# A fused top-k attention and SwiGLU kernel: the softmax weights from Exp of the bare scores, and one VectorE operation that compares, multiplies and sums

## The chip, the cores and the metric

The kernel runs on one core of a Trainium2 chip. The metric is the time of one launch on the device in microseconds (us), lower is better. The core has a TensorE for matrix products (PE in the profile, with its weight loads as PEld), a VectorE (DVE), a ScalarE (ACT), a GpSimd (POOL) and a SyncE (SP) that issues most transfers. Each engine works through its own list of instructions in order; they wait for each other by semaphores.

## The reference

There are 8 batches of 8 heads, 576 queries and keys, and a head dimension of 64. Each query keeps the scores that reach its 32nd largest; their softmax weighs the values. The 4608 x 512 result goes through a SwiGLU block with a hidden size of 1536.

```python
scores = scale * np.matmul(q, k.transpose(0, 1, 3, 2))
kth = np.partition(scores, -top_k, axis=-1)[..., -top_k:-top_k + 1]      # top_k = 32
scores = np.where(scores >= kth, scores, -1000000000.0)
attn = np.exp(scores - np.max(scores, axis=-1, keepdims=True))
attn = attn / (np.sum(attn, axis=-1, keepdims=True) + 1e-09)
x = np.matmul(attn, v)              # then (B, H, S, D) -> (B*S, H*D)
g = x @ w_gate
out = (g * (1.0 / (1.0 + np.exp(-g))) * (x @ w_val)) @ w_out
```

## The kernel before

**Units and turns.** The attention is cut into 160 units: a batch, one of five query tiles, and a pair of heads. Four of the five tiles have 128 queries and give "full" units with two heads of 128 x 576 scores each. The fifth has 64 queries, and packs both heads into one 128 x 576 tile (a "one-head" unit for VectorE). So there are 128 full and 32 one-head units, 288 tiles of 128 x 576 in all. The main loop (`for n in range(NU + 3)`, L747) makes one turn per unit, and each turn writes instructions for several units at different stages.

**The stages of a unit.** `scores` multiplies q by k into PSUM and ScalarE copies the result to the tile `sc` (L308, L313). `select` (L316) finds the 32nd largest score of each row on VectorE: four rounds of MAX8 (L328) with three MATCH_REPLACE8 (L332) between them, in which the eight values found are overwritten by a very low number. A MATCH_REPLACE8 is preceded in the profile by a small MATCH_VALUE_LOAD. The last operation of `select` is the TENSOR_SCALAR of L338: it compares the scores with the 32nd and gives 0 or a penalty. `penalize` (L342) adds the penalty to the scores on GpSimd (L350) and makes the bias of the exponential there (L348). `weigh` (L353) takes the Exp on ScalarE, which also sums it (L359), and adds the 1e-9 (L364). `normalize` (L367) takes the reciprocal on VectorE (L371) and scales the weights on ScalarE (L374). `turn` transposes them on TensorE (L386) and ScalarE copies them out (L387). `values` multiplies by v (L420), and ScalarE copies to `xT` (L436), the input of the SwiGLU block.

**Where the stages stand.** In turn n VectorE does the top-k of unit n. The penalty and Exp of unit n-1 stand at the beginning of turn n, its reciprocal at the end of turn n, its scaling at the start of turn n+1 and its transposes in turn n+1 (`TURN = 2`). The products with v come for two units at a time, for n-4 and n-3 in every even turn n.

**The SwiGLU block** (`feed`) works on 18 blocks of 256 tokens. It is cut into pieces, each a few matmuls, and `pieces(k)` writes up to k pieces into a turn as long as a credit lasts. `share(n)` (L694) sets the credit of a turn, from a fixed budget (7.0, later 6.4) less the cost of the other TensorE work of that turn. ScalarE takes the results out of PSUM and GpSimd multiplies them (L504, L509); these steps wait in the lists `on_act` and `on_pool` until a `flush` writes them. The program order is therefore fixed by hand, and at the end of the kernel every engine is tied to this order. The w matrices are rounded during the first turns by ScalarE, VectorE (L121) and GpSimd (L122, L123).

Of the kernel before, what the change touches and what calls it, by code (L numbers as in the profile page):

```python
# [8 lines left out]
AF = mybir.ActivationFunctionType  # L9
ALU = mybir.AluOpType  # L10
FP32 = mybir.dt.float32
# [4 lines left out]
P = 128  # L16
TOP_K = 32
LOWEST = -3.4028234663852886e38
FAR = -3.0e38
EPS = 1.0e-9  # L20
# [5 lines left out]
def kernel(  # L26
# [37 lines left out]
    nc = tc.nc  # L64
    B, H, S, D = q.shape
# [10 lines left out]
    scale = 1.0 / float(D) ** 0.5  # L76
    assert D == 64 and R == 64 and H * D == DM and DM == 512 and B * S % BLK == 0

    consts = ctx.enter_context(tc.tile_pool(name="consts", bufs=1))
    ld = ctx.enter_context(tc.tile_pool(name="ld", bufs=2))  # L80
    slabs = ctx.enter_context(tc.tile_pool(name="slabs", bufs=4))
    work = ctx.enter_context(tc.tile_pool(name="work", bufs=2))
    small = ctx.enter_context(tc.tile_pool(name="small", bufs=3))
# [9 lines left out]
    for i in range(NV):  # L93
        vt = consts.tile([P, P], FP32, name=f"vlast{i}")
        nc.vector.memset(vt[:], 0.0)
        vlast.append(vt)
    eps = consts.tile([P, 1], FP32, name="eps")
    nc.vector.memset(eps[:], EPS)
    wg = consts.tile([P, KC, DFF], FP32, name="wg")
    wv = consts.tile([P, KC, DFF], FP32, name="wv")  # L100
    wo = consts.tile([P, MC, DM], FP32, name="wo")
# [94 lines left out]
    early = [lambda: None]  # L196
# [4 lines left out]
    def rounding(n):  # L201
        for _ in range(n):
            next(weight, None)
# [68 lines left out]
    state = {}  # L272

    def n_heads(qt):

        return 1 if qt == J else 2
# [39 lines left out]
    def select(n):  # L316

        nh = n_heads(units[n][1])
        sc = state[n]["sc"]
        m = small.tile([P, 2, TOP_K], FP32, tag="m", name="m", bufs=2)  # L320
        heads = [slice(t * S, (t + 1) * S) for t in range(nh)]
        e = work.tile([P, 2 * S], FP32, tag="e", name="e", bufs=3)
        state[n] |= dict(m=m, e=e, heads=heads)
        cur = sc
        rounds = TOP_K // 8
        for r in range(rounds):
            for t, hs in enumerate(heads):
                nc.vector.max(m[:, t, 8 * r : 8 * r + 8], cur[:, hs])  # L328
                yield
            if r < rounds - 1:  # L330
                for t, hs in enumerate(heads):
                    nc.vector.match_replace(  # L332
                        e[:, hs], m[:, t, 8 * r : 8 * r + 8], cur[:, hs], LOWEST
                    )
                    yield
                cur = e
        for t, hs in enumerate(heads):
            nc.vector.tensor_scalar(  # L338
                e[:, hs], sc[:, hs], m[:, t, TOP_K - 1 : TOP_K], FAR, ALU.is_lt, ALU.mult
            )  # L340

    def penalize(n):  # L342

        st = state[n]
        sc, m, e, heads = st.pop("sc"), st.pop("m"), st["e"], st["heads"]
        nh = len(heads)
        bias = small.tile([P, 2], FP32, tag="bias", name="bias")
        nc.gpsimd.tensor_scalar_mul(bias[:, 0:nh], m[:, 0:nh, 0], -scale)  # L348
        every = slice(0, nh * S)
        nc.gpsimd.tensor_tensor(e[:, every], e[:, every], sc[:, every], ALU.add)  # L350
        st["bias"] = bias

    def weigh(n):  # L353

        st = state[n]
        e, heads, bias = st["e"], st["heads"], st.pop("bias")
        tot = small.tile([P, 2], FP32, tag="tot", name="tot")
        for t, hs in enumerate(heads):
            nc.scalar.activation(  # L359
                e[:, hs], e[:, hs], AF.Exp, bias=bias[:, t : t + 1], scale=scale,  # L360
                accum_out=tot[:, t : t + 1],
            )
        nh = len(heads)
        nc.scalar.activation(tot[:, 0:nh], tot[:, 0:nh], AF.Identity, bias=eps[:])  # L364
        st["tot"] = tot

    def normalize(n):  # L367
        st = state[n]
        tot, e, heads = st.pop("tot"), st["e"], st.pop("heads")
        nh = len(heads)  # L370
        nc.vector.reciprocal(tot[:, 0:nh], tot[:, 0:nh])  # L371
        yield
        for t, hs in enumerate(heads):
            nc.scalar.mul(e[:, hs], e[:, hs], tot[:, t : t + 1])  # L374

# [82 lines left out]
    def flush(queue):  # L458
        while queue:
            queue.pop(0)()  # L460
# [201 lines left out]
    NU = len(units)  # L662
# [3 lines left out]
    def piece():  # L666

        if len(on_act) > 1:
            flush(on_act)
        if len(on_pool) > 1:  # L670
            flush(on_pool)
        while True:
            if not current:
                if not todo or done.get(todo[0], 0) < NHP * BLK:
                    return 0
                flush(on_act)
                flush(on_pool)
                current.append(feed(todo.pop(0)))
            cost = next(current[0], 0)
            if cost == 0:  # L680
                current.pop()
                continue
            return cost

    def fetch(n):

        b, qt, hp = units[n]
        i = b * NHP + hp
        if qt == 0:
            yield from prep(i)  # L690
        if qt == J and i + NHP < len(pairs):
            load(i + NHP)

    def share(n):  # L694


        others = 0.0
        costs = [(m, 0.7) for m in scored(n) + valued(n)] + [(n - TURN, 0.6)]
        for m, cost in costs:
            if m >= 0:  # L700
                others += cost * (0.5 if units[m][1] == J else 1)
        if units[n + 3][1] == 0:
            others += 0.6

        beside = 6.4 if T[1] else 7.0
        return beside * n_heads(units[n][1]) / 2 - others

    def scored(n):

        ahead = [n + 1] if n < 2 else [] if n % 2 else [n + 1, n + 2]  # L710
        return [m for m in ahead if m < NU]

    def valued(n):

        behind = [] if n % 2 else [n - 4, n - 3]
        return [m for m in behind if 0 <= m < NU]

    def pieces(n):
        for _ in range(n):
            if credit[0] >= 1:  # L720
                credit[0] -= piece()

    def run(steps):
        for _ in steps:
            pass

    def finish_units(ns):
        values(ns)
        for n in ns:
            b, qt, hp = units[n]  # L730
            if qt == J and b + 1 < B:
                load_v((b + 1) * NHP + hp)
# [8 lines left out]
    load(2)  # L741
    credit = [0.0]
    no = iter(())
    scaled = no
    TURN = 2
    due = [2.0]
    for n in range(NU + 3):  # L747
        nh = n_heads(units[n][1]) if n < NU else 1
        topk = select(n) if n < NU else no
        norm = normalize(n - 1) if 0 <= n - 1 < NU else no  # L750
        nxt = [scores(m) for m in scored(n)]
        ahead = fetch(n + 3 if n else 2) if n + 3 < NU else no

        def dve(k, beside=True):

            for _ in range(k * nh):
                next(topk, None)
                due[0] += 5 / 6 if beside else 0
                if due[0] >= 1:
                    due[0] -= 1  # L760
                    rounding(1)

        if n >= NU - NHP:
            credit[0] = 8.0
        else:
            credit[0] = min(credit[0] + share(n), share(n) + 1)
        flush(on_act)
        if 0 <= n - 1 < NU:
            penalize(n - 1)
        flush(on_pool)  # L770
        run(scaled)
        if nxt:
            run(nxt.pop(0))
        if valued(n):
            finish_units(valued(n))
        if nxt:
            next(nxt[0])
        early[0]()
        if 0 <= n - 1 < NU:
            weigh(n - 1)  # L780
        if nxt:
            run(nxt.pop())


        dve(2, beside=False)
        if n == 0:
            run(ahead)
            load(3)
            ahead = fetch(3)
        if n < NHP:  # L790
            load_v(n)
        pieces(2)
        flush(on_act)
        dve(1)
        dve(1)
        if 0 <= n - TURN < NU:
            run(turn(n - TURN))

        flush(on_pool)
        next(ahead, None)  # L800
        pieces(1)
        next(ahead, None)
        dve(1)
        pieces(1)
        dve(2, beside=False)
        run(topk)
        next(norm, None)
        scaled = norm
        pieces(6)
    while piece():  # L810
        pass
# [48 lines left out]
```

## Time and profile before

| what | us |
|---|---|
| time, median of 3 runs | 1794.11 (1790.79 to 1795.02) |
| profiled execution, its own time | 1794.33 |
| its span, first to last instruction | 1792.1 |
| TensorE busy | 1691.1 (94%) |
| VectorE busy | 1619.1 (90%) |
| ScalarE busy | 1204.8 (67%) |
| GpSimd busy | 1043.2 (58%) |

The span is the profiled execution's first to last instruction; the 2.2 us between it and the execution's own time lie around it. A group line names the line of the code, the engine, the operation, the output tile and its inputs, how often it ran, the busy time and the mean duration of one in ns, and the engine's idle time before it with what ended it. A timeline line has its start and length in us, then the same names; several neighbours of a kind are merged, with their number behind the x.

### The profile page before, as it was taken

To read this page: it belongs to the slowest core of one execution; us is meant where nothing else is said; L and a number is where in the kernel's file an instruction comes from. 1 tells how busy PE (TensorE), PEld (TensorE's weight loads), DVE (VectorE), ACT (ScalarE), POOL (GpSimd) and SP (SyncE) were. 2 spreads that over 40 slices of the span, in tenths; PEclk is the share of its full clock that TensorE was granted. 3 is DMA by queue.
4 is the path that set the end of the run, shared out by engine and by line. 5 is a ranking of instruction groups with operands and counts; after the bars stand their busy time and mean duration, and the time that the engine had idled before them with its cause. 6 is when DMAs were issued, how large, how long until landed. Compare 5 with 4: busy or idle time off the path is not lost.

```text
span 1792.1 us, 30800 instructions
## 1 busy us (share of the span) xinstructions
PE 1691.1 (94%) x11012; PEld 1398.6 (78%) x11012; DVE 1619.1 (90%) x3372; ACT 1204.8 (67%) x2881; POOL 1043.2 (58%) x930
## 2 busy tenths in 40 slices
PE   4558999799999999999999999999999999999999
PEld 3337678688888888888888878888887878888877
DVE  7999999999999999998999999998999989999400
ACT  6778676667667676667666675767676676676431
POOL 4878756455565646565556546555556555656434
PEclk7569999899999999999999999999999999999989
DMA  7433130001200030001200020000300020000000
GB/s 193 128 94 94 32 75 14 13 1 36 60 1 13 2 81 14 13 1 32 64 13 1 13 70 26 1 13 4 92 1 13 1 49 21 13 1 13 1 12 12
DMA packets 109305, 59.66 MB, mean 33 GB/s; under 512 B 88544, under 2 KB 96992, under 8 KB 109152
## 3 DMA queue, kind: packets, MB, share of 16 engines
q1 hardware_dynamic: 108016, 57.37, 12.3%
q8 instruction: 87, 1.43, 0.3%
q14 instruction: 66, 0.54, 0.1%
q10 hardware_dynamic: 1136, 0.33, 0.1%
HBM read 48.23 MB, written 9.44 MB: 32 GB/s over the span
## 4 chain that ended last, share of the span: by engine, by line
PE 79%; DVE 12%; ACT 4%; POOL 3%; issue 1%; DMA 1%; SPq 0%; ACTq 0%; POOLq 0%; DVEq 0%
PE f L476 40%; PE x_ps L562 8%; PE av L420 8%; PE s L308 7%; PE etps L386 6%; PE y_ps L562 5%; DVE m L328 5%; DVE e L332 5%; PE s L294 2%; DVE e L338 1%; PE kqps L263 1%; PE o_ps L522 1%; ACT e L359 1%; POOL e L350 1%; DVE size L121 1%
## 5 line engine op out<-in xcount | busy, mean ns | idle before, releaser
L328 DVE MAX8 m<-e 128x8 f32<-128x576 f32 x864 | 614.9, 747 | 3.3
L350 POOL TENSOR_TENSOR e<-e,sc 128x1152 f32<-128x1152 f32 (+1 forms) x160 | 382.9, 2393 | 131.6 <-DVE tot L371 110.0
L332 DVE MATCH_REPLACE8 e<-m,e 128x576 f32<-128x576 f32 x576 | 423.5, 741 | 0.0
L476 PE MATMUL f<-xT,wg 128*128 128x256 f32 x1728 | 403.9, 383 | 0.0
L476 PE MATMUL f<-xT,wv 128*128 128x256 f32 x1728 | 399.6, 380 | 0.0
L476 PEld LDWEIGHTS f<-xT,wg 128*128 128x128 f32 x1728 | 325.2, 192 | 52.0 <-issue 9.2
L476 PEld LDWEIGHTS f<-xT,wv 128*128 128x128 f32 x1728 | 323.0, 190 | 49.1 <-issue 7.9
L504 POOL TENSOR_TENSOR h<-h,half_g 128x512 f32<-128x512 f32 x108 | 139.7, 1293 | 284.8 <-ACT h L503 283.0
L359 ACT ACTIVATE e<-e,bias 128x576 f32<-128x576 f32 x288 | 221.9, 775 | 113.4 <-POOL e L350 113.3
L386 PE MATMUL etps<-ident,e 128*128 128x128 f32 (+1 forms) x1312 | 185.1, 284 | 48.1 <-ACT e L374 33.5
L374 ACT ACTIVATE e<-e,tot 128x576 f32<-128x576 f32 x288 | 210.7, 780 | 22.1 <-DVE tot L371 21.8
L509 POOL TENSOR_TENSOR h<-h,val 128x512 f32<-128x512 f32 x108 | 139.2, 1289 | 148.0 <-ACT val L508 146.9
L386 PEld LDWEIGHTS etps<-ident,e 128*128 128x128 f32 (+1 forms) x1312 | 157.2, 145 | 80.3 <-POOL e L350 30.1
L308 PE MATMUL s<-kqT 64*128 64x288 f32 x1024 | 181.2, 461 | 37.3 <-ACT sc L313 22.0
L332 DVE MATCH_REPLACE8 e<-m,sc 128x576 f32<-128x576 f32 x288 | 211.6, 741 | 0.0
L328 DVE MAX8 m<-sc 128x8 f32<-128x576 f32 x288 | 202.6, 739 | 9.2 <-ACT sc L313 9.2
L387 ACT COPY et<-etps 128x512 f32<-128x512 f32 (+1 forms) x448 | 182.5, 483 | 36.3 <-PE etps L386 36.2
L338 DVE TENSOR_SCALAR e<-sc,m 128x576 f32<-128x576 f32 x288 | 182.8, 671 | 1.2
L313 ACT COPY sc<-s 128x288 f32<-128x288 f32 x512 | 164.8, 407 | 19.0 <-PE s L308 18.7
L308 PEld LDWEIGHTS s<-kqT 64*128 64x128 f32 x1024 | 102.0, 198 | 85.2 <-ACT sc L313 27.3
L420 PE MATMUL av<-et,v 128*64 128x128 f32 (+1 forms) x2560 | 162.6, 271 | 0.0
L420 PEld LDWEIGHTS av<-et,v 128*64 128x64 f32 x2560 | 140.8, 143 | 7.2 <-issue 3.4
(73 smaller groups left out, 1979.3 us busy)
## 6 DMA issues: line engine op xcount, KB each, us to landing
v<-in_v_dram SPq DMA_DIRECT2D x32, 256.0 KB, 3.2
kq_in<-in_k_dram SPq DMA_DIRECT2D x63, 128.0 KB, 3.0
kq_in<-in_q_dram SPq DMA_DIRECT2D x63, 128.0 KB, 3.2
w<-in_moe_w_gate_dram SPq DMA_DIRECT2D x12, 512.0 KB, 3.8
w<-in_moe_w_val_dram SPq DMA_DIRECT2D x12, 512.0 KB, 3.7
w<-in_moe_w_out_dram SPq DMA_DIRECT2D x12, 512.0 KB, 3.6
out_dram<-o SPq DMA_DIRECT2D x38, 128.0 KB, 2.4
out_dram<-o SPq DMA_DIRECT2D x16, 256.0 KB, 2.4
```

The source lines that it names most:

```text
L308: nc.tensor.matmul(ps[:, 0:half], slab[d, q0 : q0 + P], slab[d, k0 : k0 + half])
L328: nc.vector.max(m[:, t, 8 * r : 8 * r + 8], cur[:, hs])
L332: nc.vector.match_replace(e[:, hs], m[:, t, 8 * r : 8 * r + 8], cur[:, hs], LOWEST)
L338: nc.vector.tensor_scalar(e[:, hs], sc[:, hs], m[:, t, TOP_K - 1 : TOP_K], FAR, ALU.is_lt, ALU.mult)
L350: nc.gpsimd.tensor_tensor(e[:, every], e[:, every], sc[:, every], ALU.add)
L359: nc.scalar.activation(e[:, hs], e[:, hs], AF.Exp, bias=bias[:, t : t + 1], scale=scale, accum_out=tot[:, t : t + 1],)
L374: nc.scalar.mul(e[:, hs], e[:, hs], tot[:, t : t + 1])
L386: nc.tensor.transpose(ps[0:kl, c * P : (c + 1) * P], e[:, k0 : k0 + kl], ident[:])
L387: nc.scalar.copy(et[0:kl, c0 : c0 + cn, :], ps[0:kl, 0 : cn * P].rearrange("p (c j) -> p c j", c=cn),)
L420: nc.tensor.matmul(av[d, i, 0:ql], weights_, moving, start=c == (0 if last else J), stop=c == (J if last else J - 1),)
L476: nc.tensor.matmul(ps[:, i, :], w[:, kc, m * P : (m + 1) * P], x[:, kc, :], start=(kc == 0), stop=(kc == KC - 1),)
L562: nc.tensor.matmul(ps, lhsT, T[i][m], start=m == 0, stop=m == MQ - 1)
```

## The change

The scores are exponentiated without the penalty, for all 576 keys, on ScalarE while VectorE is still looking for the 32nd largest: `weigh(n)` moves into turn n, behind the first round of MAX8, which gives the largest score for the bias. The top-k rounds get a tile of their own, `rest`, since `e` now holds the exponentials. The last operation of `select` becomes a `scalar_tensor_tensor` with two tensor inputs: it compares the scores with the 32nd, multiplies the 0 or 1 by the exponential and writes the row's sum to `tot`. The penalty's addition on GpSimd is gone, and so are the sum and the addition of 1e-9 on ScalarE; the latter becomes a small GpSimd operation. The reciprocal and the scaling of unit n-1 move to turn n, behind two VectorE operations per head, and its transposes to turn n (`TURN = 1`). The products with v are for n-3 and n-2, in odd turns, and the scores for two units are also made in odd turns. In even turns three pieces of the SwiGLU block stand ahead of the transposes in place of two.

```diff
-    eps = consts.tile([P, 1], FP32, name="eps")
-    nc.vector.memset(eps[:], EPS)
...
+        rest = work.tile([P, 2 * S], FP32, tag="rest", name="rest", bufs=1)
         e = work.tile([P, 2 * S], FP32, tag="e", name="e", bufs=3)
+        tot = small.tile([P, 2], FP32, tag="tot", name="tot")
...
                     nc.vector.match_replace(
-                        e[:, hs], m[:, t, 8 * r : 8 * r + 8], cur[:, hs], LOWEST
+                        rest[:, hs], m[:, t, 8 * r : 8 * r + 8], cur[:, hs], LOWEST
                     )
...
-            nc.vector.tensor_scalar(
-                e[:, hs], sc[:, hs], m[:, t, TOP_K - 1 : TOP_K], FAR, ALU.is_lt, ALU.mult
+            nc.vector.scalar_tensor_tensor(
+                e[:, hs], sc[:, hs], m[:, t, TOP_K - 1 : TOP_K], e[:, hs],
+                ALU.is_ge, ALU.mult, accum_out=tot[:, t : t + 1],
             )
...
-    def penalize(n):
+    def weigh(n):
...
         nc.gpsimd.tensor_scalar_mul(bias[:, 0:nh], m[:, 0:nh, 0], -scale)
-        every = slice(0, nh * S)
-        nc.gpsimd.tensor_tensor(e[:, every], e[:, every], sc[:, every], ALU.add)
...
             nc.scalar.activation(
-                e[:, hs], e[:, hs], AF.Exp, bias=bias[:, t : t + 1], scale=scale,
-                accum_out=tot[:, t : t + 1],
+                e[:, hs], sc[:, hs], AF.Exp, bias=bias[:, t : t + 1], scale=scale
             )
-        nh = len(heads)
-        nc.scalar.activation(tot[:, 0:nh], tot[:, 0:nh], AF.Identity, bias=eps[:])
...
     def normalize(n):
...
+        nc.gpsimd.tensor_scalar_add(tot[:, 0:nh], tot[:, 0:nh], EPS)
+        yield
         nc.vector.reciprocal(tot[:, 0:nh], tot[:, 0:nh])
-        yield
         for t, hs in enumerate(heads):
             nc.scalar.mul(e[:, hs], e[:, hs], tot[:, t : t + 1])
...
-        ahead = [n + 1] if n < 2 else [] if n % 2 else [n + 1, n + 2]
+        ahead = [n + 1, n + 2] if n % 2 else [] if n else [1]
...
-        behind = [] if n % 2 else [n - 4, n - 3]
+        behind = [n - 3, n - 2] if n % 2 else []
...
-    TURN = 2
+    TURN = 1
...
         flush(on_act)
-        if 0 <= n - 1 < NU:
-            penalize(n - 1)
         flush(on_pool)
-        run(scaled)
+        next(norm, None)
         if nxt:
             run(nxt.pop(0))
         if valued(n):
             finish_units(valued(n))
         if nxt:
             next(nxt[0])
-        early[0]()
-        if 0 <= n - 1 < NU:
-            weigh(n - 1)
+        dve(1, beside=False)
+        if n < NU:
+            weigh(n)
+        dve(1, beside=False)
+        run(norm)
         if nxt:
             run(nxt.pop())
-        dve(2, beside=False)
+        early[0]()
...
-        pieces(2)
+        pieces(2 + (n + 1) % 2)
...
         run(topk)
-        next(norm, None)
-        scaled = norm
         pieces(6)
```

More of the change, by code (lines that the diff above doesn't have):

```diff
@@ L321, in select @@
         heads = [slice(t * S, (t + 1) * S) for t in range(nh)]
+        rest = work.tile([P, 2 * S], FP32, tag="rest", name="rest", bufs=1)
         e = work.tile([P, 2 * S], FP32, tag="e", name="e", bufs=3)
-        state[n] |= dict(m=m, e=e, heads=heads)
+        tot = small.tile([P, 2], FP32, tag="tot", name="tot")
+        state[n] |= dict(m=m, e=e, heads=heads, tot=tot)
         cur = sc
@@ L332, in select @@
                     nc.vector.match_replace(
-                        e[:, hs], m[:, t, 8 * r : 8 * r + 8], cur[:, hs], LOWEST
+                        rest[:, hs], m[:, t, 8 * r : 8 * r + 8], cur[:, hs], LOWEST
                     )
                     yield
-                cur = e
+                cur = rest
         for t, hs in enumerate(heads):
-            nc.vector.tensor_scalar(
-                e[:, hs], sc[:, hs], m[:, t, TOP_K - 1 : TOP_K], FAR, ALU.is_lt, ALU.mult
+            nc.vector.scalar_tensor_tensor(
+                e[:, hs], sc[:, hs], m[:, t, TOP_K - 1 : TOP_K], e[:, hs],
+                ALU.is_ge, ALU.mult, accum_out=tot[:, t : t + 1],
             )
-    def penalize(n):
+    def weigh(n):
         st = state[n]
-        sc, m, e, heads = st.pop("sc"), st.pop("m"), st["e"], st["heads"]
+        sc, m, e, heads = st["sc"], st["m"], st["e"], st["heads"]
         nh = len(heads)
@@ L348, in penalize @@
         nc.gpsimd.tensor_scalar_mul(bias[:, 0:nh], m[:, 0:nh, 0], -scale)
-        every = slice(0, nh * S)
-        nc.gpsimd.tensor_tensor(e[:, every], e[:, every], sc[:, every], ALU.add)
[L351 to L357, printed above, removed]
         for t, hs in enumerate(heads):
             nc.scalar.activation(
-                e[:, hs], e[:, hs], AF.Exp, bias=bias[:, t : t + 1], scale=scale,
-                accum_out=tot[:, t : t + 1],
-            )
-        nh = len(heads)
-        nc.scalar.activation(tot[:, 0:nh], tot[:, 0:nh], AF.Identity, bias=eps[:])
-        st["tot"] = tot
+                e[:, hs], sc[:, hs], AF.Exp, bias=bias[:, t : t + 1], scale=scale
+            )
     def normalize(n):
@@ L743 @@
     no = iter(())
-    scaled = no
-    TURN = 2
+    TURN = 1
     due = [2.0]
```

## The prediction

> **What bounds the kernel now.** I read the page's busy times and slices first, then the busy times by stretch.
>
> ```profile
> PE 1691.1 (94%) x11012; PEld 1398.6 (78%) x11012; DVE 1619.1 (90%) x3372; ACT 1204.8 (67%) x2881; POOL 1043.2 (58%) x930
> ...
> PE   4558999799999999999999999999999999999999
> ...
> DVE  7999999999999999998999999998999989999400
> ```
>
> ```profile
> 600.00:800.00 200.00, 198.69 (x1356) 166.57 (x1355) 196.41 (x410) 138.23 (x340) 117.13 (x108) 1.00 0.10 25
> 1400.00:1600.00 200.00, 197.89 (x1344) 165.53 (x1344) 192.22 (x405) 139.21 (x339) 114.21 (x102) 1.00 0.07 19
> ```
>
> The columns of the second fence are PE, PEld, DVE, ACT and POOL. From 10 to about 1655 us VectorE and TensorE are both full: 96 to 98% and 99%. ScalarE (69%) and GpSimd (58%) are not. The balance is made by the credit: a turn gets as many SwiGLU pieces as fit beside its top-k. A saving on VectorE therefore finds TensorE full, while an addition on VectorE lengthens every turn, because the pieces per turn are written into the program. The rest, about 135 us after 1657, is SwiGLU work of TensorE with almost no VectorE.
>
> Next the VectorE groups in the stretch from 0 to 1655 us, one line of code by itself, and the timeline of two ends of a turn: an undisturbed one (VectorE alone) and a disturbed one.
>
> ```profile
> L338 DVE TENSOR_SCALAR e<-sc,m 128x576 f32<-128x576 f32 x284 | 179.6, 669 | 1.0
> ...
> L371 DVE RECIPROCAL tot<-tot 128x2 f32<-128x2 f32 (+1 forms) x155 | 24.1, 155 | 18.8 <-ACT tot L364 18.8
> L332 DVE MATCH_VALUE_LOAD e<-m,sc 128x8 f32 x285 | 22.1, 78 | 21.3 <-PE etps L386 18.5
> ```
>
> ```profile
> L338 DVE TENSOR_SCALAR e<-sc,m x288: 492/514/1860, 23.0 to 1700.7; 128x576 f32<-128x576 f32 x144
> ```
>
> ```profile
> 1647.64 1.40 DVE L328 MAX8 m<-e 128x8 f32<-128x576 f32 x2
> 1648.97 0.95 DVE L338 TENSOR_SCALAR e<-sc,m 128x576 f32<-128x576 f32 x2
> 1649.84 0.15 DVE L371 RECIPROCAL tot<-tot 128x2 f32<-128x2 f32 x1
> ```
>
> ```profile
> 801.49 1.40 DVE L338 TENSOR_SCALAR e<-sc,m 128x576 f32<-128x576 f32 x2
> 801.67 0.90 POOL L548 TENSOR_TENSOR p<-p 128x256 f32<-128x256 f32 x1 [0.89 <-ACT p L596]
> ...
> 802.81 0.15 DVE L371 RECIPROCAL tot<-tot 128x2 f32<-128x2 f32 x1
> ```
>
> Two MAX8 of 576 elements take 1.33 us of the path from start to next start (1647.64 to 1648.97); two TENSOR_SCALAR of the same length take 0.87 (to 1649.84). So the operation that goes is the cheapest pass over a tile that VectorE has. Its median is 514 ns and its mean 669: beside some GpSimd operations it takes up to 1860.
>
> **The change part by part.** The sum is made against the profiled execution (1794.33 us, span 1792.1, 2.2 around it), which lies 0.2 us above the median.
>
> 1. *The last operation of the top-k* (144 pairs' worth: 128 full units and 32 single tiles). It gets a second tensor input and a sum. What it takes is in no row. Nearest are the other passes over 576 elements, MAX8 (747 ns) and MATCH_REPLACE8 (741 ns), at one element per 1.04 to 1.3 ns. The tensor-tensor operation at the end (L631, one input from PSUM, 426 ns for 256 elements) agrees: with MATCH_REPLACE8's 741 for 576, 0.98 ns per element more. So I take MAX8's pace, 1.33 us a pair. The sum must be written out. Before, ScalarE paid an extra instruction of 196 ns for that (ACTIVATION_READ_ACCUMULATOR, 56.4 us for 288); VectorE's small MATCH_VALUE_LOAD costs 78 and about 0.07 of the path. I take 0.07, the same engine's, and keep 0 and 0.196 as ends. Pair: 1.33 + 0.14 = 1.47, less the 0.87 removed: +0.60 us, times 144 = +86 us.
>
> 2. *The disturbance by GpSimd.* The whole run's group has 182.8 us busy; 288 undisturbed ones at 465 ns (half of a pair's 0.93) would be 134. So the disturbance costs 49 us. The operations beside which it happens are mostly the SwiGLU multiplications, weight rounding early on, and L548 sums, as at 801.67: they stay. The penalty L350 (382.9 us) goes, but it stands at the start of a turn, mostly not beside L338. I keep the 49 us as they are: change 0, ends -49 (the new form isn't disturbed) and +49 (exposed twice, being longer).
>
> The Trainium skill ("SBUF — State Buffer", Who interferes with whom) has TENSOR_SCALAR in a two-port mode and any VectorE operation with two SBUF inputs both locked out while GpSimd reads; by it the disturbance stays, as I take it. A rule that speaks harder against this change is in "Vector Engine (DVE) Microarchitecture Reference", Points that are easy to get wrong: this operation form with two SBUF sources that are not bf16 halves throughput. By that the pair would take about 1.2 us more; no row here shows such an operation, and the sum goes by the rows above.
>
> 3. *Waits that go.* To 1655 us VectorE waits 18.8 us for ScalarE's total (L371 <- L364) and 21.3 us ahead of the first MATCH_VALUE_LOAD of a unit, 18.5 of it until TensorE's transposes free an `e` tile. The sum now comes from VectorE itself, and `rest` needs no transposes. But the reciprocal now waits for GpSimd's 1e-9, and the last operation for Exp and its `e` tile. The first MAX8 pair, bias (0.26), two Exp (1.55) and latencies end some 4 us into a turn; the last operation stands 9.6 us into it, so that is covered unless ScalarE is held up over 5 us. I take half of the 40: -20 us, ends -40 and 0.
>
> 4. *ScalarE and GpSimd.* Gone: 288 accumulator reads (56.4 us) and 160 Identity (47.3); 160 penalties (382.9). New: 160 additions of 1e-9 at about 0.26 us (the bias L348's row, 263 ns), 42 us. All costed at nothing: ScalarE has 30% and GpSimd 40% of every stretch free. If the cover went, it would be by order, not by load: see the second rival.
>
> 5. *One turn less.* The products with v come a turn earlier, so the first blocks start and the last blocks end one turn earlier. A full turn holds about 11 us of TensorE work, some 70% SwiGLU: 8 us leave the part after the last top-k. Ends 0 and -11 (a whole turn). The loads of v that `finish_units` issues on SP and the stores move with it; the DMA row never exceeds 0.1 of the engines past 200 us in the stretches above. The moved rounding step `early`, the removed memset (59 ns) and three pieces for two change no amount of work: 0. TensorE now reaches the transposes of n-1 in turn n; in even turns three pieces of 1.89 us stand ahead, in odd turns two with the scores and values (9 us), against a reciprocal 2.9 us and a scaling some 4.6 us into VectorE's turn: covered, if the reciprocal is on time.
>
> Sum: +86 + 0 - 20 - 8 = +58 on 1794.3: 1852, say 1850.
>
> **The rivals.**
>
> *Faster.* The new operation is not disturbed (-49 on the +86), its sum costs nothing on the path (-20), and all 40 us of waits go with 8 to 11 at the end: +17 - 40 - 10 = -33, 1761; with part of it, 1765 to 1788. For it: GpSimd loses a third of its work, and VectorE's idle time has just these names. Against: the multiplications that disturb stay. It decides once items 1 and 2 cost under 28 us together.
>
> *A wait behind GpSimd's queue.* The 1e-9 stands in GpSimd's list behind the SwiGLU multiplications flushed at the start of the turn, and VectorE's reciprocal, with all the rest of the top-k behind it, and then scaling and transposes, wait for it.
>
> ```profile
> POOL h L504 <- ACT h L503: 283.0, 84, 14.2
> ```
>
> ```profile
> 817.60 0.60 ACT L501 ACTIVATE h<-f 128x512 f32<-128x512 f32 x1 [1.03 <-PE f L476]
> ...
> 818.57 0.63 ACT L503 ACTIVATE h<-h 128x512 f32<-128x512 f32 x1
> ...
> 819.28 1.28 POOL L504 TENSOR_TENSOR h<-h,half_g 128x512 f32<-128x512 f32 x1 [1.17 <-ACT h L503]
> ```
>
> From the matmuls' end to the end of the multiplication is 3.0 us (817.60 to 820.56), plus 0.26: 3.3 against 2.9 of cover. If TensorE ends the last product of a turn more than 0.4 us before VectorE's turn starts, nothing is lost; later, all of it. At 1 us on half of the 160 turns: 80 us more, 1930. Against: the transposes bind TensorE to this turn too, so it should run less behind.
>
> *Half pace.* If each of 576 elements takes twice the 0.98 ns, 0.57 us x 288 = 163 us more: 2013. For and against it no row speaks.
>
> **How the numbers follow.** A measurement here can tell about 0.3% (5.4 us) from no change. Chances: forecast 0.52 (own range 1815 to 1895, by the read-out's and the disturbance's ends), the wait 0.15, half pace 0.12, faster 0.15, and a sum that cancels within 0.3% 0.06. Slower is 0.52 + 0.15 + 0.12 = 0.79. The range 1775 to 1935 takes in the wait's 1930 and most of the faster case; it leaves out half pace and the faster case's tail, under 0.2.
>
> **What would show it.** Step 1: the new operation's own row at 700 to 780 ns undisturbed, and a small read-out near 70. Step 2: its mean 100 to 200 ns above its median. Step 3: idle time ahead of the reciprocal and of the last operation below 25 us to the end of the top-k. TensorE's busy share falls to 95 to 97% in the middle stretches. Step 5: VectorE's last top-k to the end, 8 us shorter. I am wrong if the operation holds pace with the removed one, if the reciprocal's idle time is tens of us, or if the two engines' balance hides an addition on VectorE.

## The result, and the profile after

The changed kernel takes 1879.88 us (median of 4 runs, 1876.39 to 1884.39) beside 1792.71 us before (median of 4) on the same chip: a ratio of 1.0487, with a 95% interval of 1.0459 to 1.0515. Its profiled span is 1876.7 us, 84.6 us longer than the 1792.1 before. The predicted time was 1850 us.

From the page of the changed kernel, the busy times and two rows of slices, and then two stretches in its middle (columns PE, PEld, DVE, ACT, POOL):

```profile
PE 1708.8 (91%) x11012; PEld 1391.2 (74%) x11012; DVE 1725.0 (92%) x3659; ACT 1134.6 (60%) x2433; POOL 720.0 (38%) x930
...
PE   5468999799999999999999999999999999899989
...
DVE  7999999998999999999999999999999999999520
```

```profile
600.00:800.00 200.00, 189.99 (x1287) 155.87 (x1287) 195.51 (x415) 121.54 (x267) 72.07 (x99) 0.99 0.10 25
1400.00:1600.00 200.00, 190.99 (x1263) 156.32 (x1260) 193.78 (x414) 123.29 (x269) 67.45 (x96) 0.99 0.08 19
```

ScalarE and GpSimd got the relief that the change gives them: 70 and 323 us less busy time. VectorE got 106 us more and is full in both stretches. TensorE is no longer full: 95% where it had 99%. The chain of work that ended last, followed back from the last instruction, went mostly through TensorE before (79%), and goes more through VectorE (47%) than through any other engine now (the kernel before first):

```profile
PE 79%; DVE 12%; ACT 4%; POOL 3%; issue 1%; DMA 1%; SPq 0%; ACTq 0%; POOLq 0%; DVEq 0%
```

```profile
DVE 47%; PE 32%; ACT 7%; POOL 7%; issue 7%; DMA 1%; SPq 0%; DVEq 0%; POOLq 0%; ACTq 0%
```

The VectorE groups of the whole run, by line:

```profile
L338 DVE SCALAR_TENSOR_TENSOR e<-sc,m,e 128x576 f32<-128x576 f32 x288 | 292.8, 1049 | 4.3
...
L361 DVE RECIPROCAL tot<-tot 128x2 f32<-128x2 f32 (+1 forms) x160 | 24.8, 155 | 61.5 <-POOL tot L359 61.4
L338 DVE DVE_READ_ACCUMULATOR e<-sc,m,e 128x1 f32 x288 | 23.1, 80 | 0.0
L332 DVE MATCH_VALUE_LOAD rest<-m,sc 128x8 f32 x288 | 22.0, 76 | 1.1
```

The spread of the new operation, from the view of its line (shortest, median, longest in ns):

```profile
L338 DVE SCALAR_TENSOR_TENSOR e<-sc,m,e x288: 790/815/1890, 22.2 to 1804.8; 128x576 f32<-128x576 f32 x144
L338 DVE DVE_READ_ACCUMULATOR e<-sc,m,e x288: 73/78/97, 22.9 to 1805.5; 128x1 f32 x144
```

And the timeline of two turn ends, the first undisturbed (no GpSimd operation beside the new one), the second with GpSimd at work:

```profile
829.54 1.41 DVE L328 MAX8 m<-rest 128x8 f32<-128x576 f32 x2
830.87 0.80 DVE L338 SCALAR_TENSOR_TENSOR e<-sc,m,e 128x576 f32<-128x576 f32 x1
831.60 0.08 DVE L338 DVE_READ_ACCUMULATOR e<-sc,m,e 128x1 f32 x1
831.60 0.81 DVE L338 SCALAR_TENSOR_TENSOR e<-sc,m,e 128x576 f32<-128x576 f32 x1
832.34 0.08 DVE L338 DVE_READ_ACCUMULATOR e<-sc,m,e 128x1 f32 x1
832.34 1.41 DVE L328 MAX8 m<-sc 128x8 f32<-128x576 f32 x2
```

```profile
818.68 0.81 DVE L338 SCALAR_TENSOR_TENSOR e<-sc,m,e 128x576 f32<-128x576 f32 x1
818.83 1.78 POOL L498 TENSOR_TENSOR h<-h,val 128x512 f32<-128x512 f32 x1
...
819.41 1.81 DVE L338 SCALAR_TENSOR_TENSOR e<-sc,m,e 128x576 f32<-128x576 f32 x1
...
821.16 1.41 DVE L328 MAX8 m<-sc 128x8 f32<-128x576 f32 x2
```

Undisturbed, the two operations and their read-outs take 1.47 us of the path (830.87 to 832.34), where the removed pair took 0.87. Disturbed, the second one takes 1.81 in place of 0.81, and GpSimd's multiplication, whose median is 1.27, takes 1.78: both stand still for a while. The times fit one waiting for the other: the multiplication starts 0.6 us before the first operation is done (818.83 to 819.41) and is 0.5 too long; the second operation starts 1.2 us before the multiplication is done (819.41 to 820.61) and is 1.0 too long.

Where the 84.6 us come from, cut where the fourth-last top-k ends (unit 156, the first of the last four one-head units: 1657.2 us before, 1756.9 after):

| | before | after | difference |
|---|---|---|---|
| VectorE busy up to there | 1599.1 | 1704.0 | +104.9 |
| VectorE idle up to there | 58.1 | 52.9 | -5.2 |
| from there to the end | 134.9 | 119.8 | -15.1 |

The two rows of busy times behind this table, with the same columns as above, the kernel before first:

```profile
0.00:1657.20 1657.20, 1563.70 (x10328) 1288.99 (x10330) 1599.08 (x3331) 1159.35 (x2787) 983.87 (x866) 0.96 0.14 35
```

```profile
0.00:1756.90 1756.90, 1597.59 (x10403) 1296.34 (x10404) 1704.00 (x3617) 1101.34 (x2369) 668.74 (x870) 0.96 0.13 33
```

The +104.9 can be split. The pace is 0.60 to 0.62 us per pair (a whole undisturbed turn takes 11.18 us, as from 821.16 to 832.34 above, in place of 10.56), over 142.5 pairs up to unit 156: 86 to 88. The rest is the disturbance: 288 operations at a mean of 1049 ns against an undisturbed 810 are 69 us, 20 more than the 49 that the prediction took for the kernel before. By one reckoning for both kernels (mean less median, times 288) it goes from 45 to 67, 22 more. Against these stand some 4 us that the rounding of the weights on VectorE takes less (26.0 us in L121 before, 21.6 in L119 now). The idle time has changed places: 21 us ahead of the first MATCH_VALUE_LOAD are gone (1.1 left), and the reciprocal's wait, now for GpSimd, has grown from 18.8 to 30.9 in this part; the rest of its 61.5 is in the last four units.

```profile
L361 DVE RECIPROCAL tot<-tot 128x2 f32<-128x2 f32 (+1 forms) x156 | 24.2, 155 | 30.9 <-POOL tot L359 30.7
```

### The profile page after: what moved, and what is told of

Its sections match the earlier page's. It is cut to its first block, busy times and chain, and to the rows that moved or that the text cites. A ratio compares the mean times of both kernels' runs of the same rounds, so it can differ in the third digit from the quotient of the medians.

```text
span 1876.7 us, 30744 instructions
## 1 busy us (share of the span) xinstructions
PE 1708.8 (91%) x11012; PEld 1391.2 (74%) x11012; DVE 1725.0 (92%) x3659; ACT 1134.6 (60%) x2433; POOL 720.0 (38%) x930
## 4 chain that ended last, share of the span: by engine, by line
DVE 47%; PE 32%; ACT 7%; POOL 7%; issue 7%; DMA 1%; SPq 0%; DVEq 0%; POOLq 0%; ACTq 0%
DVE m L328 21%; DVE rest L332 18%; PE f L465 14%; DVE e L338 6%; PE x_ps L551 4%; PE av L409 3%; PE etps L375 3%; PE y_ps L551 3%; ACT e L351 2%; PE s L306 2%; ACT e L363 2%; POOL h L599 1%; POOL p L537 1%; PE s L292 1%; PE o_ps L511 1%
## 5 line engine op out<-in xcount | busy, mean ns | idle before, releaser
L328 DVE MAX8 m<-rest 128x8 f32<-128x576 f32 x864 | 613.3, 746 | 2.2
L332 DVE MATCH_REPLACE8 rest<-m,rest 128x576 f32<-128x576 f32 x576 | 423.6, 741 | 0.0
L351 ACT ACTIVATE e<-sc,bias 128x576 f32<-128x576 f32 x288 | 209.7, 772 | 262.4 <-POOL bias L349 262.1
L375 PE MATMUL etps<-ident,e 128*128 128x128 f32 (+1 forms) x1312 | 196.2, 289 | 127.4 <-ACT e L363 125.4
L338 DVE SCALAR_TENSOR_TENSOR e<-sc,m,e 128x576 f32<-128x576 f32 x288 | 292.8, 1049 | 4.3
L493 POOL TENSOR_TENSOR h<-h,half_g 128x512 f32<-128x512 f32 x108 | 147.1, 1362 | 357.2 <-ACT h L492 356.4
L498 POOL TENSOR_TENSOR h<-h,val 128x512 f32<-128x512 f32 x108 | 140.8, 1303 | 214.7 <-ACT val L497 204.8
L332 DVE MATCH_REPLACE8 rest<-m,sc 128x576 f32<-128x576 f32 x288 | 211.5, 740 | 0.0
L306 PE MATMUL s<-kqT 64*128 64x288 f32 x1024 | 173.9, 451 | 18.3 <-ACT sc L311 6.8
L306 PEld LDWEIGHTS s<-kqT 64*128 64x128 f32 x1024 | 96.8, 195 | 65.4 <-issue 24.8
L359 POOL TENSOR_SCALAR tot<-tot 128x2 f32<-128x2 f32 (+1 forms) x160 | 35.0, 219 | 224.0 <-DVE e L338 217.6
```

The lines of the kernel that those rows point to most:

```text
L306: nc.tensor.matmul(ps[:, 0:half], slab[d, q0 : q0 + P], slab[d, k0 : k0 + half])
L332: nc.vector.match_replace(rest[:, hs], m[:, t, 8 * r : 8 * r + 8], cur[:, hs], LOWEST)
L338: nc.vector.scalar_tensor_tensor(e[:, hs], sc[:, hs], m[:, t, TOP_K - 1 : TOP_K], e[:, hs], ALU.is_ge, ALU.mult, accum_out=tot[:, t : t + 1],)
L351: nc.scalar.activation(e[:, hs], sc[:, hs], AF.Exp, bias=bias[:, t : t + 1], scale=scale)
L375: nc.tensor.transpose(ps[0:kl, c * P : (c + 1) * P], e[:, k0 : k0 + kl], ident[:])
L493: on_pool.append(lambda: nc.gpsimd.tensor_mul(h[:], h[:], half[:]))
```

## The experiments

Two theories were to be told apart. The first: the last operation's form (pace and disturbance) makes VectorE's path longer, and VectorE's path is the time. The rival: it is the shorter chain, with a new wait behind GpSimd's small addition or of TensorE for the scaled weights. All times below are medians beside runs of the kernel before on the same chip (1792.75 to 1793.88).

**The new order with the old form.** The mask goes to `rest`, which nobody reads; the total is taken from the 32nd score.

```diff
-            nc.vector.scalar_tensor_tensor(
-                e[:, hs], sc[:, hs], m[:, t, TOP_K - 1 : TOP_K], e[:, hs],
-                ALU.is_ge, ALU.mult, accum_out=tot[:, t : t + 1],
+            nc.vector.tensor_scalar(
+                rest[:, hs], sc[:, hs], m[:, t, TOP_K - 1 : TOP_K], FAR, ALU.is_lt, ALU.mult
             )
...
-        nc.gpsimd.tensor_scalar_add(tot[:, 0:nh], tot[:, 0:nh], EPS)
+        last = st["m"][:, 0:nh, TOP_K - 1]
+        nc.gpsimd.tensor_scalar_add(tot[:, 0:nh], last, EPS)
```

> The changed kernel with its new order, but the last operation of the top-k in the old form (one tensor input, no sum; the mask goes to a tile that nobody reads). Left out: the multiplication by the mask and the sum (the total is taken from the 32nd score), so the weights are not the reference's. Theory (the form of the operation costs the time): 0.62 us less per pair x 144 = 89 us, and the disturbance back from 69 to about 48 us: 1880 - 89 - 21 = 1770, between 1755 and 1790, below the kernel before. Rival (the shorter chain costs it: TensorE waits 124 us for the scaled weights): the waits stay and the time stays above 1850.

Measured: 1814.51 us, 1.0121 (1.0105 to 1.0136) of before. 65 us of the change's 87 are the form, but 22 stay: the forecast of 1755 to 1790 fell, and so did the rival's time above 1850. VectorE's groups in this run:

```profile
L338 DVE TENSOR_SCALAR rest<-sc,m 128x576 f32<-128x576 f32 x288 | 188.4, 690 | 1.1
...
L361 DVE RECIPROCAL tot<-tot 128x2 f32<-128x2 f32 (+1 forms) x160 | 24.8, 155 | 101.1 <-POOL tot L359 101.0
```

Its undisturbed turn is back at 10.56 us, and the time won is partly spent ahead of the reciprocal: 68.4 us up to unit 156, where the changed kernel has 30.9. A faster VectorE arrives earlier at a wait whose end others set; in the changed kernel a good half of this wait is hidden under the slow operation.

**The new form in the old order.** The penalty comes from a constant tensor, and a sum is written that nobody reads.

```diff
+    far = consts.tile([P, S], FP32, name="far")
+    nc.vector.memset(far[:], FAR)
...
-            nc.vector.tensor_scalar(
-                e[:, hs], sc[:, hs], m[:, t, TOP_K - 1 : TOP_K], FAR, ALU.is_lt, ALU.mult
+            nc.vector.scalar_tensor_tensor(
+                e[:, hs], sc[:, hs], m[:, t, TOP_K - 1 : TOP_K], far[:],
+                ALU.is_lt, ALU.mult, accum_out=some[:, t : t + 1],
             )
```

> The kernel before with one thing changed: the last operation of the top-k takes its penalty from a constant second tensor and writes out an (unused) sum; same penalty as before, same order. Theory: 89 us for the pace and 20 to 40 for the disturbance (GpSimd is busier here than in the changed kernel): 1885 to 1925. Rival (order and chain): within 20 us of 1793.

Measured: 1851.11 us, 1.0323 (1.0308 to 1.0339). VectorE's busy time rose by 98 us (1619.1 to 1717.0), but the time by 58, which is below the expected 1885 to 1925 and far above the rival's: the expectation had left out that waits shrink when VectorE is slower. The first two lines are of the kernel before, the others of this run:

```profile
L371 DVE RECIPROCAL tot<-tot 128x2 f32<-128x2 f32 (+1 forms) x160 | 24.9, 156 | 56.5 <-ACT tot L364 56.5
...
L332 DVE MATCH_VALUE_LOAD e<-m,sc 128x8 f32 x288 | 22.4, 78 | 28.1 <-PE etps L386 25.3
```

```profile
L341 DVE SCALAR_TENSOR_TENSOR e<-sc,m,far 128x576 f32<-128x576 f32 x288 | 281.6, 1009 | 1.1
...
L375 DVE RECIPROCAL tot<-tot 128x2 f32<-128x2 f32 (+1 forms) x160 | 24.9, 155 | 36.5 <-ACT tot L368 36.5
...
L335 DVE MATCH_VALUE_LOAD e<-m,sc 128x8 f32 x288 | 21.5, 75 | 7.5 <-PE etps L390 4.5
```

The reciprocal and the first MATCH_VALUE_LOAD wait 44 us where they waited 85. The form alone gives 58, the new order alone 22; together they make 80 of the 87.

**The same without the sum.** `accum_out` is dropped from the previous kernel.

> As the run of the new form in the kernel before, without the sum. Theory: the read-out's 288 x 0.078 = 22 us go, nothing else: 18 to 26 us below that run. Rival (the sum slows the operation itself): more than 40 us below it, with an operation shorter than 800 ns; second rival (the read-out is hidden): no difference.

Measured: 1849.58 us, 1.5 below, no more than the noise. The second rival holds: the read-out is hidden. The operation is as long (median 808 ns beside 812), and an undisturbed turn takes 11.16 us without the read-outs and 11.18 with them. A read-out, 78 ns long, lies under the end of the operation that it reads and does not hold up the next one: at 831.60 above, both start at the same time.

**Lighter multiplications on GpSimd.** In the changed kernel, the two SwiGLU multiplications (L493, L498) take 4 columns of each 256.

```diff
-                on_pool.append(lambda: nc.gpsimd.tensor_mul(h[:], h[:], half[:]))
+                on_pool.append(lambda: nc.gpsimd.tensor_mul(
+                    h[:, :, 0:4], h[:, :, 0:4], half[:, :, 0:4]
+                ))
```

> The changed kernel with GpSimd's two SwiGLU multiplications cut to 4 of 256 columns in each half (left out: the product on the other columns), all waits kept. Theory (the new operation stands still while GpSimd reads): the mean of the new operation falls from 1049 towards 880 ns, since these are 288 of GpSimd's 520 us of tensor work, 35 to 50 us; shorter multiplications also take some 10 to 20 us from the reciprocal's waits: 1815 to 1840. Rival (the operation's excess has another cause): its mean stays above 1000 ns and the time falls by the reciprocal's waits alone, 1860 or more.

Measured: 1825.0 us, 1.018 (1.0165 to 1.0196), in the expected range.

```profile
L338 DVE SCALAR_TENSOR_TENSOR e<-sc,m,e 128x576 f32<-128x576 f32 x288 | 249.6, 898 | 4.3
```

The operation's mean falls from 1049 to 898 ns, its median stays (810): most of the excess (42 of 67 us, mean less median) is the doing of these two multiplications; no run removes what causes the rest. VectorE's busy time falls by 45 us and its idle time by 5, which is the span's whole 50. The transposes still wait 97 us for the scaled weights, where they waited 125.

**Without the addition of 1e-9.** The line is dropped from the changed kernel, so that the reciprocal waits for VectorE alone.

> The changed kernel without GpSimd's addition of 1e-9 (left out: that addition; the sum is at least 1, since the largest score gives exp(0)), so that the reciprocal waits for no other engine. Theory (VectorE's path sets the time, 61 us of it idle ahead of the reciprocal, 30 of them before the last four units): 1840 to 1858, VectorE's busy time unchanged within 15 us. Rival (TensorE, which waits 124 us for scaled weights, binds the turn): within 10 us of 1880.

Measured: 1841.1 us, 1.027 (1.0255 to 1.0285), 39 below the changed kernel. The rival falls: the time goes down although TensorE still waits 100 us ahead of the transposes. Of the 37 us of span, 24 are idle time of VectorE and 13 busy time: the new operation is also disturbed less (mean 1013 ns). All 37 are won up to unit 156. In the last four units nothing is won: the time from there to the end is 119.7 us beside 119.8, and VectorE idles 29 us ahead of the new operation where it idled 31 ahead of the reciprocal. How such a wait comes about is seen in the changed kernel's timeline, in the first one-head turn of a batch:

```profile
661.74 1.58 POOL L493 TENSOR_TENSOR h<-h,half_g 128x512 f32<-128x512 f32 x1 [0.91 <-ACT h L492]
...
664.49 0.58 ACT L497 COPY val<-f 128x512 f32<-128x512 f32 x1 [1.71 <-PE f L465]
665.22 1.27 POOL L498 TENSOR_TENSOR h<-h,val 128x512 f32<-128x512 f32 x1 [1.91 <-ACT val L497]
666.57 0.22 POOL L359 TENSOR_SCALAR tot<-tot 128x2 f32<-128x2 f32 x1
666.82 0.17 DVE L361 RECIPROCAL tot<-tot 128x2 f32<-128x2 f32 x1 [3.10 <-POOL tot L359]
```

The sums were ready at 662.2. The 0.22 us addition stands behind a multiplication that waits for ScalarE, which waits for TensorE's product; VectorE, with its whole next top-k behind the reciprocal, stands still for 3.1 us. All 27 waits of the reciprocal in the changed kernel have this form: the addition starts 0.08 us after GpSimd's step ahead of it ends.

**The old form and no addition, in the new order.** As the first run, with the reciprocal reading the 32nd score itself.

```diff
-        nc.gpsimd.tensor_scalar_add(tot[:, 0:nh], last, EPS)
...
-        nc.vector.reciprocal(tot[:, 0:nh], tot[:, 0:nh])
+        nc.vector.reciprocal(tot[:, 0:nh], st["m"][:, 0:nh, TOP_K - 1])
```

> The new order with the old form of the last operation and no 1e-9: the reciprocal takes the 32nd score, which VectorE itself has made (left out: the mask, the sum and the 1e-9). Theory (the 1814 us of the old form in the new order are the 101 us that VectorE waits for GpSimd's small addition): 1765 to 1790, below the kernel before. Rival (the transposes, a turn earlier, bind TensorE): VectorE's idle time moves to other waits, 1800 or more.

Measured: 1789.05 us, 0.9974 (0.9962 to 0.9986). The time falls by 25 us to the upper end of the range; the 101 us of waiting are not all won. TensorE is nearly full again, and VectorE now waits for scores:

```profile
600.00:800.00 200.00, 197.78 (x1317) 165.82 (x1316) 192.62 (x404) 128.88 (x281) 70.55 (x89) 1.00 0.10 25
```

```profile
L328 DVE MAX8 m<-sc 128x8 f32<-128x576 f32 x288 | 206.0, 755 | 69.8 <-ACT sc L297 47.6 <-ACT sc L311 21.9
```

So the new order by itself, freed of the addition, is worth 4 us, although ScalarE and GpSimd have 450 us less to do in this run than before. Up to unit 156 it is even 3 us longer than the kernel before (1660.3 beside 1657.2); the part behind is 8 shorter (126.6 beside 134.9). TensorE, at 99% in this stretch, is the other bound, right behind VectorE.

**The product on GpSimd.** VectorE turns the scores into 0 or 1 in place with the old form, GpSimd multiplies the exponentials by it, at the head of its list in the turn, and the total is the sum of the Exp of the 32 largest scores.

```diff
-            nc.vector.scalar_tensor_tensor(
-                e[:, hs], sc[:, hs], m[:, t, TOP_K - 1 : TOP_K], e[:, hs],
-                ALU.is_ge, ALU.mult, accum_out=tot[:, t : t + 1],
+            nc.vector.tensor_scalar(
+                sc[:, hs], sc[:, hs], m[:, t, TOP_K - 1 : TOP_K], 1.0, ALU.is_ge, ALU.mult
             )
...
-        nc.gpsimd.tensor_scalar_add(tot[:, 0:nh], tot[:, 0:nh], EPS)
+        nc.gpsimd.tensor_tensor(e[:, every], e[:, every], sc[:, every], ALU.mult)
+        for t in range(nh):
+            nc.scalar.activation(
+                best[:], m[:, t], AF.Exp, bias=bias[:, t : t + 1], scale=scale,
+                accum_out=tot[:, t : t + 1],
+            )
...
+        next(norm, None)
         flush(on_act)
         flush(on_pool)
-        next(norm, None)
```

> A version of the new order that keeps VectorE's old form: it turns the scores into a 0 or 1 in place; GpSimd multiplies the exponentials by it, first in its list in the turn; the total is ScalarE's Exp of the 32 largest scores with its sum (left out: the 1e-9). Theory (VectorE's turn is back at 10.56 us plus some 48 us of disturbance, the reciprocal is free of GpSimd): 1765 to 1795. Rival (the product is late and the transposes wait for it): above 1800.

Measured: 1861.08 us, 1.0381 (1.0366 to 1.0397): a miss. VectorE's busy time is back (1617.2 us), but it idles 122.8 us ahead of the reciprocal, for ScalarE's sum, and TensorE's transposes wait 112 us for the scaled weights.

```profile
L369 DVE RECIPROCAL tot<-tot 128x2 f32<-128x2 f32 (+1 forms) x160 | 25.5, 160 | 122.8 <-ACT best L364 122.8
```

**The comparison on GpSimd too.** The in-place 0 or 1 is made by `nc.gpsimd.tensor_scalar` in place of VectorE's operation.

> As the run with the product on GpSimd, with the comparison there too, so that VectorE has no last operation at all. Theory: VectorE's turn falls by 0.87 us to 9.7 and loses the disturbance, 170 us in all; TensorE (1691 us of work, 73 us idle in the first 200) is then the only bound: 1740 to 1780. Rival (some 5 us per unit of GpSimd ahead of the scaling and of the SwiGLU multiplications are too late for the transposes): above 1800.

Measured: 2336.25 us, 1.303 (1.3008 to 1.3052): a plain miss, on the rival's side. GpSimd's groups, different shapes kept apart:

```profile
L361 POOL TENSOR_SCALAR sc<-sc,m 128x576 f32<-128x576 f32 x288 | 636.7, 2219 | 35.9 <-DVE m L328 15.3 <-ACT e L349 10.4 <-ACT et L386 4.2
L364 POOL TENSOR_TENSOR e<-e,sc 128x1152 f32<-128x1152 f32 x128 | 336.4, 2628 | 10.7
```

The comparison takes 2.2 us per head there, so a full unit needs 7.1 us of GpSimd (two comparisons and the product) before its weights can be scaled; the reciprocal waits 702 us. TensorE, whose granted clock is 0.88 in this run and 0.95 to 0.98 in the others, is busy for 1838.7 us with the same matmuls.

**The addition first in GpSimd's list.** One line of the changed kernel is moved, nothing left out.

```diff
+        next(norm, None)
         flush(on_act)
         flush(on_pool)
-        next(norm, None)
```

> The changed kernel with one line moved: the addition of 1e-9 goes into GpSimd's list ahead of the SwiGLU multiplications flushed at the start of the turn, nothing is left out. Theory (the reciprocal's 61 us are GpSimd's queue, not the addition itself): the wait is nearly gone and the time is that of the kernel without the addition, 1838 to 1850. Rival (the addition and its two semaphore hops cost it): 1860 or more.

Measured: 1837.12 us, 1.0245 (1.023 to 1.0261), 43 us below the changed kernel: the time came within 1 us of the expected range, the way was not the expected one.

```profile
L338 DVE SCALAR_TENSOR_TENSOR e<-sc,m,e 128x576 f32<-128x576 f32 x288 | 259.4, 932 | 4.7 <-PE s L292 0.6
...
L361 DVE RECIPROCAL tot<-tot 128x2 f32<-128x2 f32 (+1 forms) x160 | 24.5, 153 | 54.8 <-POOL tot L359 54.8
```

The wait is still 54.8 us: 23.0 up to unit 156, where it was 30.9, and 31.8 behind it. First in the turn is not first in the queue: steps that were put into GpSimd's list late in the turn before still stand ahead of the addition, as the SwiGLU multiplications of L493 do, behind which 24.9 of these 54.8 us lie. What fell is the disturbance: the new operation's mean went from 1049 to 932 ns, 33 us in all. The multiplications now wait until the addition behind VectorE's sum is done, so fewer of them run beside the operation that makes it: by the times in the traces, a SwiGLU multiplication overlaps 31 of the 288 operations here and 84 in the changed kernel.

**The kernel before without its 1e-9.** The Identity on ScalarE (L364) is dropped.

> The kernel before without ScalarE's addition of 1e-9 to the sums (left out: that addition; the sums are at least 1). Theory: the reciprocal waits for the Exp itself, 0.3 us earlier; of its 56 us most is in the last turns, where TensorE sets the time: 0 to 12 us below the kernel before. Rival (VectorE's waits are worth their full length): 20 us or more below.

Measured: 1789.9 us, 0.9981 (0.9972 to 0.999), 4 us below: within the small range expected. Of the kernels here that keep the mask and the weights it is the fastest, by a hair.

**No addition and lighter multiplications.** The two edits above together, in the changed kernel.

> The changed kernel without the addition of 1e-9 and with GpSimd's two SwiGLU multiplications cut to 4 of 256 columns in each half (left out: both). Theory (disturbance and queue are separate costs on VectorE's path): the new operation's mean near 890 ns as with the light multiplications alone, some 30 us below the kernel without the addition: 1800 to 1818. Rival (without the queue's wait TensorE binds, and a faster VectorE gains nothing): within 8 us of 1841.

Measured: 1805.83 us, 1.007 (1.0056 to 1.0084). A faster VectorE still gains: 35 us less than without the addition alone. Apart the two edits take 55 and 39 us off the changed kernel, together 74 and not 94, so disturbance and queue are two costs, but not wholly separate ones.

## Why the prediction was right or wrong

**The bound: right.** "An addition on VectorE lengthens every turn" is what the busy table shows: +104.9 us of busy time is +99.7 us at unit 156. TensorE's share in the middle fell to 95%, as the text had it. That a saving on VectorE finds TensorE full fits the run at 1789.05 us. Two limits belong to it. TensorE was not full from 10 us on: its slices show 40 to 80% up to some 180 us. And in the old order only 58 of 98 added us came through, as waits took up the rest.

**Step 1, the pace: right in sum, wrong in its terms.** +86 was forecast, 86 to 88 is measured. The pair takes the 1.47 us that were worked out, but the operation itself takes 0.73 per head, not MAX8's 0.66, and the sum's read-out almost nothing, not 0.07. Its median, 815 ns, lies above the 700 to 780 that were to show it. Two errors cancelled, and that the largest term came out right is in this part luck. The Trainium skill's rule ("Vector Engine (DVE) Microarchitecture Reference", Points that are easy to get wrong) that two SBUF sources which are not bf16 halve the throughput did not hold as the half-pace rival reads it, against the other passes over 576 elements: 815 ns beside MATCH_REPLACE8's 741 with one source. The rule does not say against what it halves; against the removed operation the pair is 1.7 times as long (1.47 us to 0.87).

**Step 2, the disturbance: the largest miss.** It was taken as unchanged at 49 us and is 69, inside the ends given (0 to 98); the mean lies 234 ns above the median, not 100 to 200. The operation is on the path for 1.47 us per pair and not 0.87, and the multiplications that disturb it stay. By mean less median (45 us before, 67 after) it is 57 with the new form in the old order and 52 with the old form in the new order: form and order both add to it. The lighter multiplications show that they cause most of it: 25 are left. "SBUF — State Buffer" of the Trainium skill, Who interferes with whom, says that a VectorE operation with two SBUF inputs contends with a GpSimd operation that reads SBUF; the 1.81 and 1.78 us side by side in the timeline agree.

**Step 3, the waits: wrong by the prediction's own sign.** -20 was forecast, -5 came up to unit 156. Below 25 us ahead of the reciprocal and the last operation were to show the step, and tens of us ahead of the reciprocal to disprove it: they are 34.8 (30.9 and 3.9). The old waits did go (the first MATCH_VALUE_LOAD from 21.3 to 1.0), but the reciprocal waits 30.9 us there, where it waited 18.8. That is the second rival's mechanism, priced at 80 us on half of the turns; it is 61.5 us over 27 turns, and removing the addition gains 39. The forecast and this rival were set up as alternatives. In fact both happened: the slower operation hides a good half of the queue's wait up to unit 156, which is 68.4 us there as soon as VectorE is fast. That the other engines catch up in the meantime is the likely reason; no run isolates it.

**Step 5, one turn less: right in sign, too small.** -8 was forecast and -15.1 measured from unit 156 to the end; from VectorE's last top-k to the end, the sign that the prediction named, it is 90.7 us before and 71.1 after. Most of it goes with the order: the old form in the new order has 121.7 us from unit 156 to the end, the new form in the old order 130.0. At unit 156 TensorE has 609 of its 11012 matmuls left where it had 684, about one turn's share (69) less. Why this is worth more than 8 us stays open.

**The sum.** +58 forecast and +84.6 measured: about 2 from the pace, 20 from the disturbance, 15 from the waits, and -7 from the end; some -4 are the weight rounding's, which no step had. The time lies inside the forecast's own range (1815 to 1895). The half-pace and the faster rival are out. For "faster", the pace alone already cost more than the 28 us at which it decided.

## What to carry to other kernels

Before an operation on the bounding engine takes over work from idle ones, price its form: here a one-input pass that was the cheapest of its kind (0.87 us a pair) became a two-input pass (1.47), and the relief of the other two engines, in the new order freed of its wait, bought 4. A small step for the bounding engine must not stand in the list of an engine behind steps that wait for something else; leaving it out gave 39 us here. Moving it ahead of the steps of its own turn took away only 8 us of its wait up to unit 156, since steps of the turn before stayed ahead; putting it on the bounding engine itself was not tried. When two engines are both full, a saving on one turns into waiting, and a cost on one eats waits first: judge a change by busy and idle time together.

## What the runs showed of the hardware

The read-out of VectorE's sum has a record of 78 ns and costs about nothing: 288 of them make 1.5 us, no more than the noise, since each lies under the operation's end. GpSimd's comparison with a per-row scalar takes 2219 ns for 128 x 576, more per element than its product of two tensors (2628 ns for 128 x 1152). And a reordering on GpSimd alone, by one line, moved VectorE's busy time by 34 us (1725.0 to 1690.5) with the same instructions on VectorE: busy time there holds the time in which it is blocked.
